# Moving loads behind a weight's bits, and four small moves at the start, in a Mamba-2 + gated MLP kernel

## The chip, the cores and the metric

The kernel runs on one core of a Trainium2 chip. The metric is the device time of one execution in microseconds. The names of the engines in the profile: PE is TensorE's matmul, PEld its weight load, DVE is VectorE, ACT is ScalarE, POOL is GpSimd, SP is SyncE, which issues nearly all DMAs here. L12 is line 12 of the kernel.

## What is computed

The reference is a chunked scan (Mamba-2, "SSD") over 4 batches x 8 heads x 768 positions with head size 32 and state size 16, then an MLP over the 3072 tokens (256 to 2048 to 256) with the quick form of Gelu between.

```python
def _attn_ref(x, a, B, C):                   # cut: set-up of shapes
    log_a = np.log(np.clip(a, 1e-06, 1.0))
    for c in range(nc):                      # chunks; xc, Bc, Cc, la are their slices
        cum = np.cumsum(la, axis=-1)
        L = np.exp(cum[:, :, :, None] - cum[:, :, None, :]) * causal
        CB = np.einsum('bhin,bhjn->bhij', Cc, Bc)
        y_intra = np.einsum('bhij,bhjd->bhid', CB * L, xc)
        y_inter = np.einsum('bhin,bhnd->bhid', Cc, state) * np.exp(cum)[:, :, :, None]
        y[:, :, sl] = y_intra + y_inter
        # ... state = decay of the whole chunk * state + sum_j decay_from_j * B_j x_j

def _moe_ref(x, w_in, w_out):                # x: y as (tokens, 256)
    h = x @ w_in
    g = h * (1.0 / (1.0 + np.exp(-1.702 * h)))
    return (g @ w_out).astype(np.float32)
```

The weights w_in and w_out come as 64-bit floats and are turned into 32-bit ones on the chip.

## The kernel before

The kernel takes the sequence in chunks of 128 positions, two chunks to a "pair" (12 pairs), two pairs to a group of 512 tokens (6 groups). A pair goes through these steps: `load` its B, C and x; `turn_only` (TensorE transposes B and C, another engine copies them out of PSUM); decays `L` (for pairs 0 and 1 by `differ` and `exps`: sums of logarithms on TensorE, Exp on ScalarE; later by scans on the DVE); `ends` (B times the decay to the chunk's end); `score` and `weigh` (C B^T, and its product with L); `gain` and `keep` (the new states); `finish` (y, two copies by ScalarE). Then the MLP: `half` and `hidden` (y times w_in, Silu), `project_all` (times w_out) for group 0, other forms for later groups, which use sums of weight blocks that `mix_in` makes. Every engine takes its instructions in the order in which the program names them (`in_order`).

Each weight comes in pieces of 64-bit words: 6 pieces of w_in (0 to 5), 4 of w_out (6 to 9). A piece goes through `fields` (DVE), `clamp` (ScalarE), `rounded` (DVE) and `join` (DVE), and join issues the load of the next piece into a buffer that has come free.

```python
    def load(p, queue=nc.sync):
        rb[p] = raw.tile([P, 2, NH, N], FP32, tag="b", name=f"b{p}", bufs=3)
        rc[p] = raw.tile([P, 2, NH, N], FP32, tag="c", name=f"c{p}", bufs=3)
        rx[p] = raw.tile([P, 2, NH, D], FP32, tag="x", name=f"x{p}", bufs=3)
        for dst, src in ((rb, B), (rc, C), (rx, x)):
            for k in range(2):
                b, c = divmod(2 * p + k, NC)
                sl = slice(c * P, (c + 1) * P)
                (queue if dst is rc else nc.sync).dma_start(out=dst[p][:, k], in_=src[b, :, sl, :].rearrange("h s d -> s h d"))
    # ...
    BUFS = 4
    bits, pieces = {}, {}
    # ... fetch(i): one DMA on nc.sync into a buffer of words(); pieces 0 and 1 share one, 2 and 3 too

    def fields(i):
        hi, cols = bits[i][1], slice(0, PIECES[i][2] * DM)
        mantissa[i] = wide.tile([P, PN], U32, tag="m", name=f"m{i}")[:, cols]
        power[i] = wide.tile([P, PN], U32, tag="p2", name=f"p2{i}")[:, cols]
        nc.vector.tensor_scalar(out=power[i], in0=hi, scalar1=0x7FF00000, scalar2=None,
                                op0=ALU.bitwise_and)
        nc.vector.tensor_scalar(out=mantissa[i], in0=hi, scalar1=0x000FFFFF,
                                scalar2=0x00100000, op0=ALU.bitwise_and, op1=ALU.bitwise_or)

    def clamp(i):
        e = power[i]
        z = e.bitcast(FP32)
        nc.scalar.activation(z, e, AF.Relu, scale=-8.0, bias=edge[:, 0:1])
        nc.scalar.activation(e, z, AF.Relu, scale=-1.0, bias=edge[:, 1:2])
    def rounded(i):
        nc.vector.scalar_tensor_tensor(out=mantissa[i].bitcast(FP32), in0=bits[i][0],
                                       scalar=2.0 ** -32, in1=mantissa[i],
                                       op0=ALU.mult, op1=ALU.add)

    NEXT = {1: (6,), 4: (7,), 5: (8,), 7: (9,)}
    def join(i):
        # ... L184: sign bits into p2 (reads the last of bits[i]); L190: product into w_in or w_out
        for n in NEXT.get(i, ()):
            fetch(n)

    def narrow(i):
        rounded(i)
        if i + 1 < len(PIECES):
            fields(i + 1)
        join(i)

```

The loads at the start, all in one queue, and the constant `idents` (the identity, 8 times, for the scans):

```python
    rows_a(az0, (nc.sync, nc.scalar))
    # ...
    load(0, nc.scalar)
    table(AF.Ln)
    fetch(0)
    load(1)
    for i in range(1, 4):
        fetch(i)
    rows_a(az, (nc.sync,))
    for i in range(4, 6):
        fetch(i)
    load(PG)
    spread_rows(1)
    # spread_rows(b): af, the raw a of batch b, for `since`; spread(n): a of chunk n from scratch
```

Copies of the transposed B and C. C goes to CT twice (Q = 2), each time times one column of `part`, a mask:

```python
        def copy(engine, o, i, scale=1.0):
            if engine == "ACT":
                nc.scalar.activation(o, i, AF.Copy, scale=scale)
            else:
                nc.vector.tensor_single_scalar(out=o, in_=i, scalar=scale, op=ALU.mult)

        s["BT"] = ssd.tile([P, 2, P], FP32, tag="BT", name=f"BT{p}")
        copy(engines[0], s["BT"], tp[:, 0])

        s["CT"] = ssd.tile([P, 2, Q, P], FP32, tag="CT", name=f"CT{p}")
        for q in range(Q):
            copy(engines[1], s["CT"][:, :, q], tp[:, 1], part[:, q:q + 1])
        s["tp"] = tp[:, 1]
        if p < PG:
            copy(engines[2], s["tp"], tp[:, 1])          # C itself, for CsT (pairs 0 and 1)
```

The order of the work at the start (`weigh` is L547, `keep` L579 and L586, `gain` L564, `half` L665 and L669; y's copies in `finish` are L631):

```python
    differ(0, [(r, ab[0, r]) for r in range(R)])
    exps(0, range(R))
    turn_only(0, ("DVE", "DVE", "DVE"))
    since_exp()
    fields(0)
    clamp(0)
    rounded(0)
    score(0, ab0)
    differ(1, [(r, ab[1, r]) for r in range(2)])
    exps(1, range(2))
    nc.gpsimd.tensor_tensor(out=own, in0=same[:, :HB], in1=same[:, HB:], op=ALU.add)
    ends(0, 0, nc.gpsimd)
    ends(0, 1, nc.gpsimd)
    weigh(0)
    turn_only(1, ("ACT", "ACT", "ACT"))
    gain(0)
    for r in range(2, R):
        ab[1, r] = bank(f"ab1_{r}")
        mask(ab[1, r])
    differ(1, [(r, ab[1, r]) for r in range(2, R)])
    exps(1, range(2, R))
    table(AF.Silu)
    since_start(0, nc.gpsimd)
    since_start(1, nc.gpsimd)
    nc.gpsimd.tensor_copy(idents, ident.unsqueeze(1).to_broadcast([P, NH, P]))
    keep(0)
    join(0)
    fields(1)
    rounded(1)
    score(1)
    ends(1, 0)
    ends(1, 1)
    weigh(1, (0,))
    finish(0)
    clamp(1)
    gain(1)
    keep(1, (0,))
    half(0, 0)
    weigh(1, (1,))
    finish(1, late=True)
    join(1)
    fields(2)
    clamp(2)
    half(1, 0)
    keep(1, (1,))
    load(PG + 1)
```

The end of y and of the first projection:

```python
    # finish(p): products y[t] (L600, L609), then
        to = early_y if p == 0 else yT[g][:, :, cols]
        for t in range(NK):
            nc.scalar.activation(to[:, t], y[t].rearrange("p k i -> p (k i)"), AF.Copy)
        if p == 0:
            nc.gpsimd.tensor_copy(yT[g][:, :, cols], to)
    # project_all: f = 0 to 15, each first the work hung in, then four products o[..] (L763); then
        for half in range(2):
            ob = out_tile(g, half)
            nc.vector.tensor_single_scalar(out=ob, in_=o[half], scalar=1.0 / GELU_SCALE,
                                           op=ALU.mult)
            store(g, half, ob)
```

What is hung into the hidden products and the projection of group 0, cut to the loads, the bits and `mix_in`:

```python
    for i, k in ((2, 1), (3, 3), (4, 4), (5, 6)):
        at(in_hidden[0], k, lambda i=i: narrow(i), lambda i=i: i < 5 and clamp(i + 1))
    at(in_hidden[0], 5, store_a)
    # store_a: clips a and writes it to scratch
    # ... k = 8, 9: pick_a(PG), clamp(6), fan_all(PG) (decays of pair 2, L384)
    at(in_hidden[0], 11, since_fanned, lambda: narrow(6))
    at(in_hidden[0], 15, lambda: clamp(7))
    for k in range(2):
        at(in_hidden[0], 5 + k, lambda k=k: spread(CG + 2 + k))
    # ...
    at(in_project[0], 9, lambda: narrow(9))
    # ...
    at(in_project[0], 14, lambda: finish(PG + 1))
    for i in range(2):
        at(in_project[0], 14, lambda i=i: mix_in(i))
    for k in range(PG):
        at(in_project[0], 8 + k, lambda k=k: load(2 * PG + k))
    for k, i in enumerate((9, 11, 13, 15)):
        at(in_project[0], i, lambda k=k: spread(2 * CG + k))
    # ... group 1:
    at(after, "H7", lambda: mix_in(2), lambda: mix_in(3))
```

Of the kernel before, what the change touches and what calls it, by code (L numbers as in the profile page):

```python
# [11 lines left out]
AF = mybir.ActivationFunctionType  # L12
ALU = mybir.AluOpType
# [3 lines left out]
P = 128  # L17
# [18 lines left out]
def kernel(  # L36
# [74 lines left out]
# [9 lines that stand above are left out]
# [51 lines left out]
# [5 lines that stand above are left out]
# [44 lines left out]
    def spread_rows(b):  # L220
        raf[b] = raw.tile([P, NC, P], FP32, tag="af", name=f"af{b}", bufs=1)
        nc.sync.dma_start(out=raf[b].rearrange("p c s -> p (c s)"),
                          in_=a[b].unsqueeze(1).to_broadcast([NH, N, S]))
# [13 lines left out]
    def table(f):  # L237

        nc.scalar.activation(early, early, f)
# [7 lines left out]
    rows_a(az, (nc.sync,))  # L247
    for i in range(4, 6):
        fetch(i)
    load(PG)  # L250
    spread_rows(1)


    edge = const.tile([P, 2], FP32, name="edge")
# [233 lines left out]
    def turn_only(p, engines=("ACT", "ACT", "ACT")):  # L488
        s = st[p] = {}
        tp = bank(f"tp{p}").rearrange("p (j k i) -> p j k i", j=2, k=2)  # L490
        for j, src in enumerate((rb[p], rc[p])):
            for k in range(2):
                nc.tensor.transpose(out=tp[:, j, k], in_=src[:, k].rearrange("p h n -> p (h n)"),  # L493
                                    identity=ident)
# [8 lines that stand above are left out]
        copy(engines[0], s["BT"], tp[:, 0])  # L503

        s["CT"] = ssd.tile([P, 2, Q, P], FP32, tag="CT", name=f"CT{p}")
        for q in range(Q):
            copy(engines[1], s["CT"][:, :, q], tp[:, 1], part[:, q:q + 1])
        s["tp"] = tp[:, 1]
        if p < PG:

            s["tp"] = ssd.tile([P, 2, P], FP32, tag="CsT", name=f"C{p}", bufs=3)
            copy(engines[2], s["tp"], tp[:, 1])
# [29 lines left out]
    def weigh(p, ks=(slice(0, 2),)):  # L542

        L, cb = Ls[p], st[p]["cb"]
        Lv = L.rearrange("p k r q i -> p k r (q i)")
        for k in ks:
            nc.vector.tensor_tensor(out=Lv[:, k], in0=Lv[:, k],  # L547
                                    in1=cb.rearrange("p r k e -> p k r e")[:, k], op=ALU.mult)
# [369 lines left out]
    def exps(p, rs):  # L918
        for r in rs:
            decay_exp(p, r, ab[p, r])  # L920
# [11 lines left out]
        mask(idle)  # L932
    differ(0, [(r, ab[0, r]) for r in range(R)])
    exps(0, range(R))
    turn_only(0, ("DVE", "DVE", "DVE"))
    since_exp()
    fields(0)
    clamp(0)
    rounded(0)
    score(0, ab0)  # L940
    differ(1, [(r, ab[1, r]) for r in range(2)])
    exps(1, range(2))
# [1 line left out]
    ends(0, 0, nc.gpsimd)  # L944
    ends(0, 1, nc.gpsimd)
    weigh(0)
    turn_only(1, ("ACT", "ACT", "ACT"))
    gain(0)
    for r in range(2, R):
# [1 line left out]
        mask(ab[1, r])  # L951
    differ(1, [(r, ab[1, r]) for r in range(2, R)])
    exps(1, range(2, R))
    table(AF.Silu)
    since_start(0, nc.gpsimd)
    since_start(1, nc.gpsimd)
    nc.gpsimd.tensor_copy(idents, ident.unsqueeze(1).to_broadcast([P, NH, P]))
    keep(0)
    join(0)
    fields(1)  # L960
    rounded(1)
    score(1)
    ends(1, 0)
    ends(1, 1)
    weigh(1, (0,))
    finish(0)
    clamp(1)
    gain(1)
    keep(1, (0,))
    half(0, 0)  # L970
    weigh(1, (1,))
    finish(1, late=True)
    join(1)
    fields(2)
    clamp(2)
    half(1, 0)
    keep(1, (1,))
    load(PG + 1)


    def at(places, i, *work):
# [17 lines left out]
    at(in_hidden[0], 15, lambda: clamp(7))  # L999
    for k in range(2):  # L1000
        at(in_hidden[0], 5 + k, lambda k=k: spread(CG + 2 + k))
    at(in_project[0], 0, lambda: turn_only(PG), lambda: narrow(7), lambda: since_start(PG))
    at(in_project[0], 1, lambda: advance(PG), lambda: clamp(8), lambda: decay(CG + 2))
    at(in_project[0], 4, lambda: scores(PG), lambda: narrow(8))
# [3 lines left out]
    at(in_project[0], 9, lambda: narrow(9))  # L1008
    at(in_project[0], 10, lambda: advance(PG + 1), lambda: scores(PG + 1))
    at(in_project[0], 14, lambda: finish(PG + 1))  # L1010
    for i in range(2):
        at(in_project[0], 14, lambda i=i: mix_in(i))
    for k in range(PG):
        at(in_project[0], 8 + k, lambda k=k: load(2 * PG + k))
# [22 lines left out]
    for k in range(CG):  # L1037
        at(after, f"P{k}", lambda k=k: decay(3 * CG + k))
        at(after, "H1" if k < 2 else "H3", lambda k=k: spread(3 * CG + k))
    at(after, "H7", lambda: mix_in(2), lambda: mix_in(3))  # L1040
    at(after, "P3", lambda: clip_rows(2), lambda: decay_rows(2), lambda: turn(p))
    at(after, "P4", lambda: mix_y(2), lambda: advance(p), lambda: turn(p + 1))
    at(after, "P5", lambda: advance(p + 1))
# [140 lines left out]
```

## Time and profile before

| | before |
|---|---|
| time, median of 3 runs | 378.24 us (377.25 to 378.48) |
| span of the profiled execution | 375.2 us |
| granted TensorE clock | 0.999 |
| DVE busy, 0 to 40 us in four tens | 4.31, 9.78, 9.67, 8.75 us |
| TensorE busy, the same | 8.61, 9.10, 9.83, 10.00 us |
| DMA busy share, the same | 0.98, 0.99, 0.84, 0.91 |
| DVE busy, 80 to 90 us | 6.35 us |

A matmul of 32-bit floats shows as two records. The records of TensorE overlap and their ends are modelled, so its busy time alone doesn't tell whether it runs at its peak; the list of its waits and the starts of its products tell more. A line of a timeline gives start, duration, engine, line and operation, out<-in, shapes, the number of instructions merged, and in brackets the idle time before it with the instruction that ended it.

### The profile page before, as it was taken

What the parts mean: (1) busy time and instruction counts of PE and PEld (TensorE: products, weight loads), DVE (VectorE), ACT (ScalarE), POOL (GpSimd) and SP (SyncE); (2) the same over time, 40 slices, a digit from 0 to 9 for tenths busy, and PEclk for the clock granted to TensorE, in tenths of its full rate; (3) what the DMA queues carried; (4) which work ended last, traced back from release to release, by engine and by line L of the source; (5) the groups of instructions that cost most, each with busy time, mean ns of one, the idle gap of its engine ahead of it and who ended that gap; (6) DMA issues with size and microseconds to landing.
All of it is one profiled execution on the core that took longest, in us unless ns stands there. A gap on an engine that the chain in (4) does not pass through costs nothing.

```text
span 375.2 us, 5771 instructions
## 1 busy us (share of the span) xinstructions
PE 367.2 (98%) x2280; PEld 284.8 (76%) x2280; DVE 268.2 (71%) x439; ACT 152.3 (41%) x337; POOL 12.4 (3%) x35
## 2 busy tenths in 40 slices
PE   8999999999999999999999999999999999999995
PEld 4674458886457678788888878888878888888884
DVE  3999899996879998677887565888574355544343
ACT  5769562403421122453423554333454331554330
POOL 4400000100000010000000000000000000000000
PEclk9999999999999999999999999999999999999999
DMA  9988888615947100077200064000010000000011
GB/s 152 235 258 194 182 307 114 190 64 91 198 93 166 59 19 23 2 142 139 112 3 0 1 114 113 0 2 0 0 58 2 0 3 1 0 2 0 0 58 56
DMA packets 85794, 29.56 MB, mean 79 GB/s; under 512 B 75720, under 2 KB 79240, under 8 KB 85768
## 3 DMA queue, kind: packets, MB, share of 16 engines
q1 hardware_dynamic: 83320, 28.81, 32.8%
q10 hardware_dynamic: 2448, 0.39, 0.6%
q8 instruction: 18, 0.29, 0.3%
q14 instruction: 8, 0.07, 0.1%
HBM read 25.95 MB, written 3.24 MB: 78 GB/s over the span
## 4 chain that ended last, share of the span: by engine, by line
PE 87%; DVE 8%; DMA 2%; issue 1%; ACT 1%; DVEq 0%; ACTq 0%
PE acc L820 32%; PE X L723 15%; PE Y L733 11%; PE o L763 8%; PE h L651 7%; PE cb L536 3%; PE y L609 3%; DMA bits<-in_moe_w_out_dram 2%; PE y L600 2%; PE tp L493 1%; DVE L L547 1%; DVE L L384 1%; PE oT L854 1%; DVE p L184 1%; PE h L665 1%
## 5 line engine op out<-in xcount | busy, mean ns | idle before, releaser
L820 PE MATMUL acc<-mg,mw 128*128 128x256 f32 x240 | 65.3, 379 | 0.0
L728 ACT ACTIVATE ac<-X 128x256 f32<-128x256 f32 x64 | 24.6, 384 | 68.9 <-PE X L723 68.8
L820 PEld LDWEIGHTS acc<-mg,mw 128*128 128x128 f32 x240 | 45.6, 190 | 6.2
L651 PE MATMUL h<-yT,w_in 128*128 128x512 f32 x112 | 50.0, 595 | 0.0
L837 DVE TENSOR_TENSOR gT<-Y,ac 128x512 f32<-128x512 f32 x32 | 22.1, 692 | 38.0 <-PE Y L733 34.9
L700 ACT ACTIVATE gT<-gT 128x512 f32<-128x512 f32 x64 | 33.3, 521 | 28.5 <-DVE gT L837 28.5
L820 PE MATMUL acc<-gT,w_out 128*128 128x256 f32 x160 | 43.8, 380 | 0.0
L349 DVE TENSOR_TENSOR_SCAN L<-a,idents 128x1024 f32<-128x1024 f32 x18 | 41.1, 2283 | 0.0
L723 PE MATMUL X<-my,mi 128*128 128x256 f32 x128 | 38.7, 384 | 0.0
L651 PEld LDWEIGHTS h<-yT,w_in 128*128 128x128 f32 x112 | 20.8, 190 | 23.4 <-issue 22.4
L820 PEld LDWEIGHTS acc<-gT,w_out 128*128 128x128 f32 x160 | 30.1, 190 | 5.4 <-issue 1.4
L837 DVE TENSOR_TENSOR gT<-Y,b 128x256 f32<-128x256 f32 x32 | 13.5, 421 | 28.0 <-PE Y L733 27.7
L654 ACT ACTIVATE gT<-h 128x512 f32<-128x512 f32 x28 | 16.6, 596 | 39.6 <-PE h L651 39.5
L763 PE MATMUL o<-w_out,gT 128*128 128x256 f32 x128 | 29.4, 384 | 0.6 <-DVE w_out L190 0.6
L547 DVE TENSOR_TENSOR L<-L,cb 128x2048 f32<-128x2048 f32 (+1 forms) x12 | 25.3, 2109 | 6.2 <-PE cb L536 6.2
L691 DVE TENSOR_TENSOR mg<-gT 128x512 f32<-128x512 f32 x40 | 27.3, 683 | 1.9 <-ACT gT L700 1.9
L763 PEld LDWEIGHTS o<-w_out,gT 128*128 128x128 f32 x128 | 23.7, 190 | 4.9 <-issue 1.1
L723 PEld LDWEIGHTS X<-my,mi 128*128 128x128 f32 x128 | 23.8, 190 | 4.2 <-issue 1.2
L820 PE MATMUL acc<-gT,mw 128*128 128x256 f32 (+1 forms) x86 | 24.0, 368 | 0.4 <-DVE c L837 0.4
L820 PE MATMUL acc<-mg,w_out 128*128 128x256 f32 x80 | 23.5, 379 | 0.0
L631 ACT ACTIVATE yT<-y 128x256 f32<-128x256 f32 x22 | 7.2, 381 | 37.6 <-PE y L609 36.3
L733 PE MATMUL Y<-yT,mi 128*128 128x256 f32 x64 | 19.5, 386 | 0.0
(145 smaller groups left out, 543.4 us busy)
## 6 DMA issues: line engine op xcount, KB each, us to landing
a<-scratch SPq DMA_DIRECT2D x18, 512.0 KB, 5.3
bits<-in_moe_w_out_dram SPq DMA_DIRECT2D x4, 1024.0 KB, 7.0
x<-in_x_dram SPq DMA_DIRECT2D x24, 128.0 KB, 3.2
out_dram<-ob SPq DMA_DIRECT2D x11, 256.0 KB, 2.2
bits<-in_moe_w_in_dram SPq DMA_DIRECT2D x4, 512.0 KB
bits<-in_moe_w_in_dram SPq DMA_DIRECT2D x2, 1024.0 KB
b<-in_B_dram SPq DMA_DIRECT2D x24, 64.0 KB, 3.9
c<-in_C_dram SPq DMA_DIRECT2D x22, 64.0 KB, 2.9
```

Of the source, the lines that this page charges most:

```text
L349: nc.vector.tensor_tensor_scan(out=Ls[p][:, k].rearrange("p r q i -> p (r q i)"), data0=ra[n], data1=idents.rearrange("p h i -> p (h i)"), ...
L547: nc.vector.tensor_tensor(out=Lv[:, k], in0=Lv[:, k], in1=cb.rearrange("p r k e -> p k r e")[:, k], op=ALU.mult)
L651: nc.tensor.matmul(out=h, lhsT=w_in[:, k, f * P:(f + 1) * P], rhs=yT[g][:, k], start=(k == 0), stop=(k == NK - 1))
L654: nc.scalar.activation(gT[g, j][:, i], h, AF.Silu, scale=GELU_SCALE)
L691: nc.vector.tensor_tensor(out=t[:, 0:2], in0=B[:, :, 1], in1=B[:, 0], op=ALU.subtract)
L700: nc.scalar.activation(o, i, AF.Silu, scale=GELU_SCALE)
L723: nc.tensor.matmul(out=s["X"], lhsT=lhsT, rhs=rhs, start=i == "1", stop=i == "4", skip_group_check=True)
L728: nc.scalar.activation(copy, s["X"], AF.Copy)
L733: nc.tensor.matmul(out=o, lhsT=lhsT, rhs=rhs, start=s.pop("new", False), stop=i != "5", skip_group_check=True)
L763: nc.tensor.matmul(out=o[k // 2][:, k % 2], lhsT=gT[g, f // 2][:, f % 2, k * P:(k + 1) * P], rhs=w_out[:, f], start=(f == 0 and k % 2 == 0 ...
L820: nc.tensor.matmul(out=acc[g][0][i][:, cols], lhsT=lhsT, rhs=rhs[:, cols], start=(j == 0 and i in (0, 2, 5, 6)), stop=(j == NF // 2 - 1), ...
L837: nc.vector.tensor_tensor(out=o, in0=v, in1=w, op=ALU.add)
```

## The change

Six moves. (1) The loads of B, C, x of pair 2 and of a of batch 1 are issued after `join(1)`, and so behind piece 6, the first of w_out, which join(1) issues; the loads of pair 3 are issued with the spreads of a, behind piece 8. The purpose is that the bits of w_out needn't stand in the queue behind loads that are needed later. (2) Where the DVE copies C (pair 0), one product with broadcast operands writes both copies. (3) `idents` is made by the DVE, before the first copies of B, in place of GpSimd, later. (4) On the DVE, `rounded(0)` goes behind weigh(0), and `rounded(1)` behind the last weigh of pair 1. (5) Silu's table is loaded behind the copies of the first y and clamp(1), not ahead of them. (6) mix_in(2) and (3) join the first two at the end of group 0's projection.

```diff
--- before.py
+++ after.py
@@ -247,8 +247,6 @@
     rows_a(az, (nc.sync,))
     for i in range(4, 6):
         fetch(i)
-    load(PG)
-    spread_rows(1)
 
 
     edge = const.tile([P, 2], FP32, name="edge")
@@ -503,8 +501,13 @@
         copy(engines[0], s["BT"], tp[:, 0])
 
         s["CT"] = ssd.tile([P, 2, Q, P], FP32, tag="CT", name=f"CT{p}")
-        for q in range(Q):
-            copy(engines[1], s["CT"][:, :, q], tp[:, 1], part[:, q:q + 1])
+        if engines[1] == "DVE":
+            nc.vector.tensor_tensor(
+                out=s["CT"], in0=tp[:, 1].unsqueeze(2).to_broadcast([P, 2, Q, P]),
+                in1=part.unsqueeze(1).unsqueeze(3).to_broadcast([P, 2, Q, P]), op=ALU.mult)
+        else:
+            for q in range(Q):
+                copy(engines[1], s["CT"][:, :, q], tp[:, 1], part[:, q:q + 1])
         s["tp"] = tp[:, 1]
         if p < PG:
 
@@ -932,11 +935,11 @@
         mask(idle)
     differ(0, [(r, ab[0, r]) for r in range(R)])
     exps(0, range(R))
+    nc.vector.tensor_copy(idents, ident.unsqueeze(1).to_broadcast([P, NH, P]))
     turn_only(0, ("DVE", "DVE", "DVE"))
     since_exp()
     fields(0)
     clamp(0)
-    rounded(0)
     score(0, ab0)
     differ(1, [(r, ab[1, r]) for r in range(2)])
     exps(1, range(2))
@@ -944,6 +947,7 @@
     ends(0, 0, nc.gpsimd)
     ends(0, 1, nc.gpsimd)
     weigh(0)
+    rounded(0)
     turn_only(1, ("ACT", "ACT", "ACT"))
     gain(0)
     for r in range(2, R):
@@ -951,31 +955,31 @@
         mask(ab[1, r])
     differ(1, [(r, ab[1, r]) for r in range(2, R)])
     exps(1, range(2, R))
-    table(AF.Silu)
     since_start(0, nc.gpsimd)
     since_start(1, nc.gpsimd)
-    nc.gpsimd.tensor_copy(idents, ident.unsqueeze(1).to_broadcast([P, NH, P]))
     keep(0)
     join(0)
     fields(1)
-    rounded(1)
     score(1)
     ends(1, 0)
     ends(1, 1)
     weigh(1, (0,))
     finish(0)
     clamp(1)
+    table(AF.Silu)
     gain(1)
     keep(1, (0,))
     half(0, 0)
     weigh(1, (1,))
     finish(1, late=True)
+    rounded(1)
     join(1)
+    load(PG)
+    spread_rows(1)
     fields(2)
     clamp(2)
     half(1, 0)
     keep(1, (1,))
-    load(PG + 1)
 
 
     def at(places, i, *work):
@@ -999,6 +1003,7 @@
     at(in_hidden[0], 15, lambda: clamp(7))
     for k in range(2):
         at(in_hidden[0], 5 + k, lambda k=k: spread(CG + 2 + k))
+    at(in_hidden[0], 6, lambda: load(PG + 1))
     at(in_project[0], 0, lambda: turn_only(PG), lambda: narrow(7), lambda: since_start(PG))
     at(in_project[0], 1, lambda: advance(PG), lambda: clamp(8), lambda: decay(CG + 2))
     at(in_project[0], 4, lambda: scores(PG), lambda: narrow(8))
@@ -1008,7 +1013,7 @@
     at(in_project[0], 9, lambda: narrow(9))
     at(in_project[0], 10, lambda: advance(PG + 1), lambda: scores(PG + 1))
     at(in_project[0], 14, lambda: finish(PG + 1))
-    for i in range(2):
+    for i in range(4):
         at(in_project[0], 14, lambda i=i: mix_in(i))
     for k in range(PG):
         at(in_project[0], 8 + k, lambda k=k: load(2 * PG + k))
@@ -1037,7 +1042,6 @@
     for k in range(CG):
         at(after, f"P{k}", lambda k=k: decay(3 * CG + k))
         at(after, "H1" if k < 2 else "H3", lambda k=k: spread(3 * CG + k))
-    at(after, "H7", lambda: mix_in(2), lambda: mix_in(3))
     at(after, "P3", lambda: clip_rows(2), lambda: decay_rows(2), lambda: turn(p))
     at(after, "P4", lambda: mix_y(2), lambda: advance(p), lambda: turn(p + 1))
     at(after, "P5", lambda: advance(p + 1))
```

## The prediction

> **What bounds the kernel now.** I read the page's busy times first, then who made TensorE wait, then the timelines of the single engines in the first 60 us, which is all the change touches apart from one move near 128 us. The page, and below it the complete list of TensorE's recorded waits:
>
> ```profile
> span 375.2 us, 5771 instructions
> PE 367.2 (98%) x2280; PEld 284.8 (76%) x2280; DVE 268.2 (71%) x439; ACT 152.3 (41%) x337; POOL 12.4 (3%) x35
> ```
>
> ```profile
> PE busy L375 <- DVE ones L258: 1.2, 1, 1.2
> PE o L763 <- DVE w_out L190: 0.6, 1, 0.6
> PE ab L536 <- DVE C L500: 0.5, 1, 0.5
> PE A L564 <- DVE Be L394: 0.5, 1, 0.5
> PE acc L820 <- DVE c L837: 0.4, 1, 0.4
> PE h L665 <- DVE w_in L190: 0.2, 1, 0.2
> ```
>
> The columns are total, times and longest, in us. TensorE sets the end: all its waits together are 3.4 us, and the change adds or removes no product. So the most that can come is what stands in this list, and the first and the fifth line (start of the program, last group) are untouched. The four in between, 1.8 us, are the candidates, and each names the DVE. Their sites, from the DVE's own timeline (start, duration, instruction; the bracket is idle time before it):
>
> ```profile
> 15.84 1.20 DVE L190 SCALAR_TENSOR_TENSOR w_in<-m,p 128x512 f32<-128x512 f32 x1
> 16.96 1.25 DVE L157 TENSOR_SCALAR p<-bits 128x512 uint32<-128x512 uint32 x1
> ...
> 19.19 0.49 DVE L394 TENSOR_TENSOR Be<-b,L 128x128 f32<-128x128 f32 x2
> ...
> 23.17 0.69 DVE L190 SCALAR_TENSOR_TENSOR w_in<-m,p 128x512 f32<-128x512 f32 x1
> 23.78 0.42 DVE L157 TENSOR_SCALAR p<-bits 128x512 uint32<-128x512 uint32 x1
> ...
> 38.92 0.69 DVE L157 TENSOR_SCALAR p<-bits 128x1024 uint32<-128x1024 uint32 x1 [1.09 <-DMA bits<-in_moe_w_out_dram]
> ...
> 51.90 1.22 DVE L190 SCALAR_TENSOR_TENSOR w_out<-m,p 128x1024 f32<-128x1024 f32 x1
> ```
>
> The reader is to see two things. The same two operations take 0.69 and 0.42 us at 23 us, but 1.20 and 1.25 us at 16 us. And at 38.92 the DVE stood 1.09 us for the bits of the second weight. GpSimd, ScalarE and the DMA queue in those stretches:
>
> ```profile
> 16.43 1.50 POOL L957 COPY idents<-ident 128x1024 f32<-128x1024 f32 x1
> ```
>
> ```profile
> 17.83 1.28 ACT L239 ACT_TABLE_LOAD   x1
> 19.13 0.20 ACT L239 ACTIVATE early<-early 128x1 f32<-128x1 f32 x1
> 19.24 0.64 ACT L631 ACTIVATE y<-y 128x256 f32<-128x256 f32 x2
> ```
>
> ```profile
> 19.19 5.15 SPq L119 DMA_DIRECT2D b<-in_B_dram  x2
> 24.39 4.05 SPq L119 DMA_DIRECT2D c<-in_C_dram  x2
> 28.48 1.31 SPq L119 DMA_DIRECT2D x<-in_x_dram  x2
> 29.83 0.90 SPq L222 DMA_DIRECT2D af<-in_a_dram  x1
> 30.85 0.38 SPq L145 DMA_DIRECT2D bits<-in_moe_w_out_dram  x1
> ```
>
> The idents copy covers the two slow DVE operations. The table load holds up the copies of the first y, which TensorE had finished at 18.99. And the first bits of w_out, whose buffer was free at 23.1 (end of L184 in join(1)), were issued at 30.85 behind pair 2's loads, and landed 8.0 us later.
>
> **What the Trainium skill says.** "Advanced Engine Details and Errata", section "GPSIMD Details": the Pool engine shares a read and a write interface with the DVE, in conflict with DVE instructions in a 2-port mode or with two SBUF inputs. The trace agrees: L190 has two SBUF inputs and lost 0.51 us, L157 lost 0.83. "VectorE: DVE Perf Modes", section "The perf-mode tier table": a copy of fp32 between SBUF tiles runs at two elements a cycle at best, and with a PSUM operand fp32 runs at one. Agrees: L300, SBUF to SBUF, took 0.55 us for 768 elements, while a single-input operation from PSUM took 0.42 for 256. "ScalarE: Activation LUTs", section "What ACT_TABLE_LOAD costs": 1283 ns for a load, plus a drain of 1380 ns. The load agrees (1.28 us); the drain isn't to be seen, since Exp ended at 17.81 and the load began at 17.83. "DMA: Bandwidth & Descriptors", section "Queues, rings and completion order": an engine takes the descriptors of a ring in order, so what is queued first goes first. The trace before shows only this one order.
>
> **The change part by part.**
>
> Start, up to TensorE's half(1,0) at 24.00. From 10.36 to 18.99 TensorE runs without a recorded gap (scores of pair 0, decays of pair 1, scores of pair 1, first y). The first of these waited for the last Exp of ScalarE (four of about 0.5 us from 8.25, end 10.32) as well as for the DVE's C copies. Making two C copies (0.78 us together) into one product of 512 elements (0.69, the duration of such a product from PSUM in L837) thus doesn't bring it forward: 0 us. The idents copy goes into the DVE's 2.05 us of idle time ahead of 8.81. It takes 0.6 to 1.2 us for 1024 elements, by L300's rate or at one a cycle: 0 us.
>
> DVE after that. weigh(0) no longer stands behind rounded(0): it needs the scores (end 11.53) and GpSimd's two Be (end 11.51), so it starts at 11.6, not 11.98, and ends at 13.87. Then rounded(0) 0.60, to 14.47; keep(0) from 14.47 (before 14.25); join(0) and fields(1), free of idents, end about 17.5, though GpSimd's CsT product (15.77 to 16.50) still runs beside join(0). Be of pair 1 waits for ScalarE's last Exp (17.81): start 17.86, where it was 19.19. From there the DVE runs: Be 0.4, weigh(1,0) 18.25 to 19.38, keep 0.6 to 20.05, weigh(1,1) 1.13 to 21.18, rounded(1) 0.60, and join(1) 0.62 + 0.70 to 23.10 (before 23.86). With the handover of 0.14 half(1,0) can start at 23.24.
>
> TensorE beside it. y(0) ends at 18.99 as before. gain(1) follows at once (before 19.53), since Be is there. ScalarE, with no table load ahead, copies y from about 18.85, as at pair 2, where the copies began 0.93 after the first of its L609. half(0,0) starts at 19.4 instead of 19.98 and ends at 21.3; y(1) takes 0.42 + 1.01 + 0.48 and ends at 23.2. DVE and TensorE arrive together at 23.25. **Gain 0.75 us.** The table load, now after clamp(1) (19.5 to 21.0), ends near 22.4, and the first Silu can have its input at 21.3: it begins about 0.4 later than before (22.02), but its bank isn't asked for until half(1,0) at 23.2.
>
> 23 to 53 us. TensorE runs on with nothing recorded but the wait at 53.27. The closest case is the weight for hidden(0,8), ready at 35.89 and used at 36.13; both move by 0.75, so the gap stays. Bits of w_out: issued at about 22.5 behind w_in's last pieces (landed by 30.85), 1 MB at the 400 GB/s or so that the DMA view shows in its best slices is 2.6 us, so landed about 33.5. The DVE asks for them at 37.83 - 0.4 = 37.4. The 1.09 wait goes. The DVE is then 1.5 us earlier, so w_out's first piece is ready near 51.6, and TensorE wants it at 52.66 - 0.75 = 51.9. **Gain 0.61 us**, all of the wait, since TensorE can win no more there than it waited.
>
> After 53 us. mix_in(2) and (3), 8 x 0.37 = 2.94 us of DVE, move from 128 us into the 3.42 us that the DVE stood ahead of the output copy at 87.59. They fit with about 0.5 us to spare. At 128 to 131 the DVE loses that load, but TensorE shows no wait there: 0 us.
>
> Sum: 378.24 - 0.75 - 0.61 = 376.88, told as 376.9.
>
> **The rivals.**
>
> First, ScalarE or TensorE instead of the DVE in the first 24 us. If the copies of y(0) start only when TensorE is quite done, half(0,0) comes at 19.77, y(1) ends at 23.56, and the start gains 0.4: about 377.2. For it: the shift of y(0) is none, and 0.2 us of slack is all there is. Against: the copies at pair 2 began while the last products ran.
>
> Second, a transfer takes the place of the old wait. Loads of pairs 2 and 3 now come 10 us later; b of pair 2 is asked for at 45.6, b of pair 3 at about 59.7, and the queue has two megabyte pieces and two spreads ahead of pair 3. The short rows are slow: issuing pair 2 took 10.6 us (19.19 to 29.83). Should they land late, the DVE stands and TensorE with it, and the 0.6 us goes back or more: 377.5 to 379. For it: the DMA engines are busy 0.77 to 0.91 of the time from 30 to 60 us. Against: pair 2 should land near 36 and pair 3 by 55, some 5 us and more ahead, and the scratch writes that held up later spreads no longer wait for pair 3.
>
> Third, the DVE at 88 us: if mix_in doesn't fit, the output copies free their banks late and TensorE waits at hidden(1): up to 1 us, 377.9. Against: 2.94 is less than 3.42.
>
> Fourth, more than the sum: if the first scores waited on C rather than on Exp, TensorE moves 0.1 to 0.2 us forward from 10.36: 376.7.
>
> **Range and chances.** Single runs of before lie 1.2 us apart, as much as the gain. The range from 375.9 to 378.2 holds the sum, the first and the third rival and that spread. A change of 2% is 7.6 us; TensorE waits only 3.4 in all, so faster by that has 0.01, slower by that needs a long DMA stall, 0.01, and the rest, 0.98, is within 2%.
>
> **What would show it.** L190 and L157 in the first 24 us at about 0.7 and 0.4; the first y copy near 18.9; half(1,0) near 23.25; the DVE without a wait for w_out's bits, and TensorE's list without L763's and L564's lines. Wrong would be a new wait in that list: for b, x or a spread between 45 and 75 us, or for the output copies near 87; also a half(1,0) that still starts at 23.6 or later, or a gap left at the first w_out product.

## The result, and the profile after

The changed kernel takes 375.71 us (median of 6 runs, 375.62 to 376.32), the kernel before 377.81 in the same comparison (6 runs, 377.25 to 378.48): ratio 0.9947, 95% interval 0.9934 to 0.9961, so 2.1 us less. The prediction of 376.9 with a range from 375.9 to 378.2 had the direction right; the time fell 0.2 us below the range.

The profiled execution of the changed kernel took 376.32 us, the longest of its six; that of the kernel before took 377.17, less than any of its six. The two traces are therefore nearer to each other (spans 374.6 and 375.2) than the medians. The page after (its last line here is the chain of work that ended last, in shares of the span):

```profile
span 374.6 us, 5767 instructions
...
PE 367.4 (98%) x2280; PEld 285.0 (76%) x2280; DVE 267.5 (71%) x439; ACT 152.3 (41%) x337; POOL 10.6 (3%) x34
...
PE 94%; DVE 3%; ACT 1%; issue 1%; DVEq 0%; ACTq 0%
```

Of the page before, the line like the last of these:

```profile
PE 87%; DVE 8%; DMA 2%; issue 1%; ACT 1%; DVEq 0%; ACTq 0%
```

TensorE's recorded waits after, the complete list (total, times, longest, in us):

```profile
PE busy L373 <- DVE ones L256: 1.2, 1, 1.2
PE ab L539 <- ACT L L474: 0.6, 1, 0.6
PE h L668 <- DVE w_in L190: 0.4, 1, 0.4
PE acc L823 <- DVE c L840: 0.4, 1, 0.4
```

(L392 is ends, which makes Be, L474 the Exp of exps, L539 score, L567 gain, L582 and L589 keep, L636 GpSimd's copy to yT, L668 half, L766 the products with w_out, L772 the output copy.) Two lines of before are gone: the first w_out product (0.6) and gain's (0.5). The scores wait 0.56, before 0.55, now for ScalarE's last Exp in place of the DVE's C copies. half's wait grew from 0.2 to 0.4. TensorE has 94% of the chain that ended last, before 87%, and the DMA no longer stands in it. The DVE's timeline at the places that the prediction named (start, duration, instruction; idle time before it in brackets):

```profile
6.91 0.68 DVE L938 COPY idents<-ident 128x1024 f32<-128x1024 f32 x1
...
16.82 1.10 DVE L190 SCALAR_TENSOR_TENSOR w_in<-m,p 128x512 f32<-128x512 f32 x1
17.84 0.41 DVE L157 TENSOR_SCALAR p<-bits 128x512 uint32<-128x512 uint32 x1
...
18.57 0.49 DVE L392 TENSOR_TENSOR Be<-b,L 128x128 f32<-128x128 f32 x2
...
20.43 0.61 DVE L589 SCALAR_TENSOR_TENSOR S<-S,since,S 128x128 f32<-128x128 f32 x1
20.96 1.21 DVE L550 TENSOR_TENSOR L<-L,cb 128x1024 f32<-128x1024 f32 x1
22.09 0.68 DVE L173 SCALAR_TENSOR_TENSOR m<-bits,m 128x512 f32<-128x512 uint32 x1
22.69 0.68 DVE L184 SCALAR_TENSOR_TENSOR p<-bits,p 128x512 uint32<-128x512 uint32 x1
23.41 0.69 DVE L190 SCALAR_TENSOR_TENSOR w_in<-m,p 128x512 f32<-128x512 f32 x1
...
37.98 0.69 DVE L157 TENSOR_SCALAR p<-bits 128x1024 uint32<-128x1024 uint32 x1
...
86.08 0.42 DVE L688 TENSOR_TENSOR mi<-w_in,mi 128x256 f32<-128x256 f32 x1
86.99 0.69 DVE L772 TENSOR_SCALAR ob<-o 128x512 f32<-128x512 f32 x1 [0.49 <-PE o L766]
```

```profile
21.05 0.35 DVE L586 SCALAR_TENSOR_TENSOR S<-S,since,S 128x128 f32<-128x128 f32 x1
```

fields(1) (L157 at 17.84) fell from 1.25 to 0.41 us, but join(0) (L190 at 16.82) only from 1.20 to 1.10, and keep's L589 at 20.43 rose from 0.35 (L586 in the line of before below) to 0.61. At 37.98 the DVE finds the bits there, where it had stood 1.09 us. Ahead of the output copy at 86.99 it has 0.49 us left of 3.42. GpSimd, ScalarE and the DMA queue beside it:

```profile
16.48 0.89 POOL L524 TENSOR_TENSOR CsT<-C,since 128x256 f32<-128x256 f32 x1 [3.89 <-ACT C L496]
20.28 0.61 POOL L636 COPY yT<-y 128x512 f32<-128x512 f32 x1 [2.91 <-ACT y L634]
```

```profile
17.45 1.09 ACT L474 ACTIVATE L<-ab 128x512 f32<-128x512 f32 x2 [1.11 <-PE ab L455]
19.56 0.66 ACT L634 ACTIVATE y<-y 128x256 f32<-128x256 f32 x2 [1.03 <-PE y L612]
...
21.60 1.28 ACT L239 ACT_TABLE_LOAD   x1
```

```profile
23.40 0.37 SPq L145 DMA_DIRECT2D bits<-in_moe_w_out_dram  x1
23.81 3.05 SPq L119 DMA_DIRECT2D b<-in_B_dram  x2
```

The two slow operations of the DVE lie beside a GpSimd instruction each: L190 beside the CsT product, L589 beside the copy to yT. The first of the two cost the chain nothing: Be of pair 1 (L392, at 18.57) has to wait for ScalarE's last Exp (end 18.54) in any case. The table load stands behind the y copies, and the bits are issued ahead of pair 2's loads. TensorE's timeline around the first w_out product, before and then after:

```profile
52.06 0.38 PE L493 MATMUL tp<-ident,b 128*128 128x128 f32 x2
52.28 0.38 PE L493 MATMUL tp<-ident,c 128*128 128x128 f32 x2
53.27 1.10 PE L763 MATMUL o<-w_out,gT 128*128 128x256 f32 x4 [0.61 <-DVE w_out L190]
```

```profile
52.31 0.38 PE L491 MATMUL tp<-ident,b 128*128 128x128 f32 x2
52.52 0.38 PE L491 MATMUL tp<-ident,c 128*128 128x128 f32 x2
52.74 1.46 PE L766 MATMUL o<-w_out,gT 128*128 128x256 f32 x6
```

From the start of the last transposes to the start of the product it was 0.99 us, and is now 0.22: 0.77 us less, where the recorded wait is 0.61, since that is counted from a modelled end.

**The accounts of the two traces.** The scores of pair 0 start at 10.36 before and at 11.08 after. Nothing in the change delays them: kernels of both kinds, below, start them anywhere from 9.93 to 11.12. When a landed and how long the first products took differ between them too. So I count from the scores. half(1,0) follows 13.64 us behind them before (24.00) and 13.17 after (24.25): 0.47 gained. The w_out product follows at 42.91 and at 41.66: 1.25 in all, and with 0.07 won within its next products the span is 1.32 us shorter for equal starts. From hidden(1,0) to the end it is 286.95 us in both.

### The profile page after: what moved, and what is told of

Same layout as the page of the kernel before. It is cut to its first block, busy times and chain, and to the rows that moved or that the text cites. A ratio compares the mean times of both kernels' runs of the same rounds, so it can differ in the third digit from the quotient of the medians.

```text
span 374.6 us, 5767 instructions
## 1 busy us (share of the span) xinstructions
PE 367.4 (98%) x2280; PEld 285.0 (76%) x2280; DVE 267.5 (71%) x439; ACT 152.3 (41%) x337; POOL 10.6 (3%) x34
## 4 chain that ended last, share of the span: by engine, by line
PE 94%; DVE 3%; ACT 1%; issue 1%; DVEq 0%; ACTq 0%
PE acc L823 32%; PE X L726 15%; PE h L654 13%; PE Y L736 11%; PE o L766 8%; PE cb L539 3%; PE y L612 3%; PE y L603 2%; PE h L668 1%; PE tp L491 1%; DVE L L550 1%; PE oT L857 1%; PE A L567 1%; PE ab L447 1%; PE ab L455 1%
## 5 line engine op out<-in xcount | busy, mean ns | idle before, releaser
L766 PE MATMUL o<-w_out,gT 128*128 128x256 f32 x128 | 29.3, 383 | 0.0
L766 PEld LDWEIGHTS o<-w_out,gT 128*128 128x128 f32 x128 | 23.8, 190 | 4.1 <-issue 0.7
```

The lines of the kernel that those rows point to most:

```text
L766: nc.tensor.matmul(out=o[k // 2][:, k % 2], lhsT=gT[g, f // 2][:, f % 2, k * P:(k + 1) * P], rhs=w_out[:, f], start=(f == 0 and k % 2 == 0 ...
```

## The experiments

Every text quoted names its own theories. What was open: (a) why the start brought 0.47 and not 0.75; (b) whether the wait of w_out is a fixed 0.61 us or a floor set by the landing of the bits, which takes away what is gained ahead of it; (c) where the rest of the 2.1 us is. A comparison runs each kernel beside the kernel before; medians of before differ from comparison to comparison, so the ratios are compared, not the times.

**The two kernels again** (e4 is before; e3 and e13 are after). No edit.

> The kernel before unchanged. Both: ratio 1.000. What its profile settles: under theory A the DVE's wait for the first w_out bits is different from the 1.09 us of the first profile, longer in a longer run, and the gap ahead of L763 follows it; under theory B it is 1.09 again and a longer run is longer before 24 us.

> The changed kernel unchanged. Both theories: 2.1 us faster than before, 375.7 us. What its profile settles: whether the late start of the profiled run (first scores at 11.08 instead of 10.36) comes back. Theory A says that it was that run's landing of a, so scores near 10.36 and a span near 374.0; theory B that part of the change delays or hastens the start, so 11.08 again.

> The changed kernel unchanged, beside the mended one. The first comparison gave it 2.1 us over before, the second 1.2. Theory A (what varies is how late w_out's bits land in before): before's median differs between the comparisons more than the changed kernel's, which stays at 375.6 to 376.1.

The kernel before against itself: 376.97 us (13 runs), ratio 1.0003 (0.9989 to 1.0018). In its profiled execution the DVE waited 0.42 us for the bits, not 1.09, and TensorE has no recorded wait at the w_out product. The changed kernel: 376.01 (20 runs) against 377.01 (48 runs), 0.9968 (0.9958 to 0.9978), and once more 375.69 (5 runs), 0.9966 (0.9954 to 0.9979). So the gain in repeats is 1.2 to 1.3 us, not the 2.1 that was expected of e3. Between the three comparisons the median of before moved by 0.80 us (377.81, 377.01, 377.19), that of the changed kernel by 0.32. The scores started at 9.93 and 10.35, half(1,0) 13.16 to 13.17 later, the w_out product 41.66 later in both, as in the first trace.

**The loads alone, and everything but the loads.** The first is the kernel before with part 1; the second is the changed kernel with the loads at their old places.

```diff
 # e1: before, with
-    load(PG)                      # ahead of the constants
-    spread_rows(1)
     join(1)
+    load(PG)
+    spread_rows(1)
     keep(1, (1,))
-    load(PG + 1)
     for k in range(2):
         at(in_hidden[0], 5 + k, lambda k=k: spread(CG + 2 + k))
+    at(in_hidden[0], 6, lambda: load(PG + 1))
 # e2: after, with the reverse of these lines
```

> The kernel before with the moved loads alone (part 1). Theory A, the wait for w_out's bits is the larger part and differs from run to run: about 1.4 us faster than before by the medians (0.85 us that the gap ahead of the first w_out product measures in the profiled runs, and some 0.6 us more that an ordinary run of before waits); half(1,0) starts as in before, 13.6 us after the first scores, and the gap ahead of L763 is gone. Theory B, the surplus comes from the start: only about 0.85 us faster.

> The changed kernel with the loads of pairs 2 and 3 back at their old places. Theory A: within 0.2 us of before although half(1,0) comes about 0.5 us earlier, because the first w_out product then waits for the same landing, and the gap there grows by as much. Theory B: 1.2 us faster than before.

The loads alone: 376.55 us, ratio 0.9985 (0.9975 to 0.9994), or 0.6 us faster, less than either theory said. The w_out product stands 42.14 us behind the scores (10.76, 52.90) and has no wait in the list. Everything but the loads: 376.92, ratio 0.9998 (0.9987 to 1.0009), though half(1,0) came 13.17 behind the scores as in the changed kernel. From that kernel's timelines, DVE and TensorE:

```profile
38.88 0.69 DVE L157 TENSOR_SCALAR p<-bits 128x1024 uint32<-128x1024 uint32 x1 [1.59 <-DMA bits<-in_moe_w_out_dram]
```

```profile
53.23 1.97 PE L768 MATMUL o<-w_out,gT 128*128 128x256 f32 x8 [1.11 <-DVE w_out L190]
```

The start was gained and lost again: the DVE came earlier and waited 1.59 us in place of 1.09, TensorE 1.11 in place of 0.61, and the product began at the same time as before (53.23 and 53.27). That is a floor, not a fixed wait. The parts don't add: 0.6 and 0.1 us alone, 1.2 together.

**Is the floor the landing?** Four more executions of the kernel before (e15 to e18), no edit:

> The kernel before, one profiled execution. Theory A: the first w_out product starts at the later of TensorE's arrival (42.1 us after the first scores) and 14.3 us after the DVE gets w_out's first bits, and the execution ends 322 us after it; in a longer execution it is the bits that come later. Theory B: the bits come at the same time in every execution (38.6 to 38.9), and a longer one is longer elsewhere.

> The same once more, for another draw of the start and of the landing: theory A and theory B as in the look before.

> The same once more: theory A and theory B as in the look before.

> The same once more: theory A and theory B as in the look before.

| execution | scores | fields(6) begins | wait for the bits | scores + 42.14 | fields(6) + 14.35 | w_out product | time |
|---|---|---|---|---|---|---|---|
| first trace | 10.36 | 38.92 | 1.09 | 52.50 | 53.27 | 53.27 | 377.17 |
| e4 | 10.76 | 38.64 | 0.42 | 52.90 | 52.99 | 53.00 | 376.88 |
| e15 | 10.72 | 39.31 | 1.12 | 52.86 | 53.66 | 53.67 | 377.56 |
| e16 | 11.08 | 38.46 | none | 53.22 | 52.81 | 53.21 | 377.04 |
| e17 | 10.63 | 38.42 | 0.32 | 52.77 | 52.77 | 52.78 | 376.68 |
| e18 | 11.12 | 38.50 | none | 53.26 | 52.85 | 53.26 | 377.08 |

The two constants are from e1 and from the first trace (so its row agrees by construction); in that trace the DVE works through the 14.2 us from fields(6) to the end of the weight without a recorded wait. The later of the two columns gives the product within 0.01 us each time, also in e16 and e18, where the bits were not waited for and the DVE was held by its own work. The landing moves by 0.9 us from execution to execution, TensorE's arrival by 0.8, and the time follows the later one. So theory A's formula holds; that the longer executions come from late bits alone doesn't: e15 was long by its bits, e16 and e18 by their start. The DVE's lines of e15 and e16:

```profile
39.31 0.69 DVE L157 TENSOR_SCALAR p<-bits 128x1024 uint32<-128x1024 uint32 x1 [1.12 <-DMA bits<-in_moe_w_out_dram]
```

```profile
38.46 0.69 DVE L157 TENSOR_SCALAR p<-bits 128x1024 uint32<-128x1024 uint32 x1
```

Then the queue itself: two transfers of 64 KB in the short rows of C, read by nobody, ahead of the bits in the kernel before (e11), and behind them in the changed one (e12).

```diff
     load(PG)
+    spare = dram.tile([2, NH, P, N], FP32, name="spare")
+    for k in range(2):
+        nc.sync.dma_start(out=spare[k].rearrange("h s d -> s h d"),
+                          in_=C[3, :, k * P:(k + 1) * P, :].rearrange("h s d -> s h d"))
     spread_rows(1)
```

> The kernel before with two more transfers of short rows (64 KB each, from C to a spare place in DRAM, read by nobody) ahead of w_out's first bits. Theory A, the landing of these bits is the bound of before: each microsecond that they land later comes out at the end; I expect 3 to 5 us later, and a time 3 to 5 us longer, with TensorE's wait ahead of L763 as much longer. Rival, the wait at L763 isn't on the path (the lost time is won back before 88 us): the same time as before.

> The changed kernel with the same two spare transfers of C as in the run with more ahead of the bits, here behind w_out's first bits, after pair 2's loads. Theory A: none of the 1.0 us that they cost in before; the DVE has no wait for the first bits, and the time is the changed kernel's. Rival, the spare transfers cost by loading the DMA engines, wherever they stand: 0.5 us or more above it.

e11: 378.48 us, ratio 1.0038 (1.0025 to 1.0050). I had expected the bits 3 to 5 us later; the DVE got them at 39.63, 0.3 to 1.2 us later than in the six executions above, and the time went up by 1.4 us in the ratio (0.0038 of 377). The two took 1.78 us to issue, where the two C loads just ahead of them took 4.01; why is not shown. The queue's line, the DVE's and TensorE's:

```profile
29.26 1.78 SPq L253 DMA_DIRECT2D spare<-in_C_dram  x2
```

```profile
39.63 0.69 DVE L157 TENSOR_SCALAR p<-bits 128x1024 uint32<-128x1024 uint32 x1 [1.37 <-DMA bits<-in_moe_w_out_dram]
```

```profile
53.98 1.97 PE L766 MATMUL o<-w_out,gT 128*128 128x256 f32 x8 [0.88 <-DVE w_out L190]
```

39.63 + 14.35 is 53.98. e12: 375.92, ratio 0.9970 (0.9957 to 0.9982), product 41.67 behind the scores: the same transfers behind the bits cost nothing. What stands ahead of the bits in the queue sets the floor.

**What held the start back.** e8 takes part 4 back (rounded(0) and rounded(1) at their old places); e9 takes the copy to yT from GpSimd and gives it to ScalarE behind half(1,0); e10 does both.

```diff
 # e8: after, with (lines between left out)
     clamp(0)
+    rounded(0)
     weigh(0)
-    rounded(0)
     fields(1)
+    rounded(1)
     finish(1, late=True)
-    rounded(1)
     join(1)
 # e9: after, with
         if p == 0:
-            nc.gpsimd.tensor_copy(yT[g][:, :, cols], to)
+            pass
     half(1, 0)
+    nc.scalar.activation(yT[0][:, :, :2 * P], early_y, AF.Copy)
```

> The changed kernel with rounded(0) and rounded(1) back at their old places on the DVE. Theory: in the changed kernel half(1,0) waits 0.40 us for the DVE; rounded(0) stands idle-free behind weigh(0) while the DVE waits 0.91 us ahead of it, so the move lengthens the DVE's chain by 0.6 us. Undone, half(1,0) starts when TensorE arrives, 12.77 us after the first scores instead of 13.17, and the time is 0.4 us below the changed kernel. Rival, the move is what brought the half microsecond: half(1,0) 13.4 or later, time 0.3 us or more above it.

> The changed kernel with GpSimd's copy of the first y into yT made by ScalarE instead, behind half(1,0)'s Silu. Theory, that copy collides with the DVE's L589 and costs it 0.26 us: L589 takes 0.35 instead of 0.61, half(1,0) starts 12.9 us after the first scores, the time is 0.25 us below the changed kernel. Rival, L589 is long for another reason (its operand S from PSUM's product): 0.61 and 13.17 as in the changed kernel.

> The changed kernel with both mends: rounded(0) and (1) at their old places, and yT copied by ScalarE. Theory, TensorE is the bound once the DVE no longer is: half(1,0) 12.8 us after the first scores, as with the first mend alone, so 0.4 us below the changed kernel and no better than with one mend. Rival, the two add up: 12.5 and 0.65 us below.

e8: 375.38 us, ratio 0.9958 (0.9942 to 0.9974); e9: 375.45, 0.9958 (0.9943 to 0.9973); e10: 375.47, 0.9959 (0.9947 to 0.9972). half(1,0) stands 12.79, 12.90 and 12.80 us behind the scores (13.17 in the changed kernel), the w_out product 41.29, 41.40 and 41.29 (41.66). Both mends together bring no more than e8. TensorE has no recorded wait at half(1,0) in the three. TensorE's line of e8 and the DVE's of e9:

```profile
23.09 1.10 PE L668 MATMUL h<-y,w_in 128*128 128x256 f32 x4
```

```profile
19.90 0.35 DVE L589 SCALAR_TENSOR_TENSOR S<-S,since,S 128x128 f32<-128x128 f32 x1
```

With no GpSimd copy beside it L589 takes 0.35 us, not 0.61: the collision is shown. join(1)'s product (L190) begins 12.33 us behind the scores in the changed kernel, 12.06 in e9, 11.96 in e10 and 11.95 in e8. So the collision costs 0.27, and the new order of the rounded operations another 0.10 without it: with the new order Be of pair 1 starts 7.49 us behind the scores (7.48 in e9), as soon as ScalarE's last Exp is over, and with the old one, behind rounded(1), at 7.98 (e8). So the move wins 0.50 ahead of Be and pays 0.60 for rounded(1) behind it. With the old order the collision is gone too, since the DVE comes to L589 at 20.13, when GpSimd's copy (19.50 to 20.11) is over. That is why e10 gains nothing over e8: its DVE chain is no shorter (11.96 and 11.95), and half(1,0) starts 0.84 behind L190 in both, as in the changed kernel. The theory of e10 had the number right for another reason. The change's part 4 lengthens the chain that it was to shorten.

**idents back on GpSimd** (e5). The changed kernel without part 3:

```diff
-    nc.vector.tensor_copy(idents, ident.unsqueeze(1).to_broadcast([P, NH, P]))
     turn_only(0, ("DVE", "DVE", "DVE"))
     since_start(1, nc.gpsimd)
+    nc.gpsimd.tensor_copy(idents, ident.unsqueeze(1).to_broadcast([P, NH, P]))
```

> The changed kernel with idents made by GpSimd again, behind the CsT products. Theory: L190 about 1.2 and L157 about 1.2 us on the DVE near 17 us, Be of pair 1 about 1.1 us later, half(1,0) 14.2 us after the first scores, the time 1.1 us above the changed kernel. Rival, the collision lies in slack: 13.2 and the same time.

376.50 us, ratio 0.9989 (0.9981 to 0.9997): without this part most of the gain is gone. half(1,0) stands 13.70 behind the scores, the w_out product 42.20, or 0.54 more than in the changed kernel. The ratios differ by about 0.8 us; 0.22 of the rest lies outside the span, below. GpSimd's line and the DVE's:

```profile
16.56 1.50 POOL L959 COPY idents<-ident 128x1024 f32<-128x1024 f32 x1
```

```profile
16.07 1.10 DVE L190 SCALAR_TENSOR_TENSOR w_in<-m,p 128x512 f32<-128x512 f32 x1
17.09 1.25 DVE L157 TENSOR_SCALAR p<-bits 128x512 uint32<-128x512 uint32 x1
```

Only L157 pays for idents (1.25, 0.41 without); L190 has its 1.10 in both. GpSimd's CsT product stands beside it in every run, and no run moved that; e19, below, is the kernel before without the idents copy on GpSimd, and has:

```profile
15.79 1.19 DVE L190 SCALAR_TENSOR_TENSOR w_in<-m,p 128x512 f32<-128x512 f32 x1
```

I had expected half(1,0) later still, 14.2 behind the scores; but the later DVE comes to L589 when the copy to yT is over, and L589 takes 0.35.

**Table, mix_in and C copies back** (e14). The changed kernel without parts 2, 5 and 6:

```diff
-        if engines[1] == "DVE":
+        if False:                 # two copies of C again
     exps(1, range(2, R))
+    table(AF.Silu)
     clamp(1)
-    table(AF.Silu)
-    for i in range(4):
+    for i in range(2):
         at(in_project[0], 14, lambda i=i: mix_in(i))
+    at(after, "H7", lambda: mix_in(2), lambda: mix_in(3))
```

> The changed kernel with three of its moves undone at once: Silu's table ahead of the first y's copies, mix_in(2) and (3) near 128 us, two copies of C. Theory: the y copies come 0.45 us later, half(0,0) 0.4 us later, but half(1,0) waited 0.40 us for the DVE anyway: 13.2 us after the first scores, the same time within 0.1 us. Rival, the table counts in full: 13.6 and 0.4 us above the changed kernel.

375.74 us, ratio 0.9969 (0.9956 to 0.9983), w_out product 41.61 behind the scores: the three parts are worth nothing on this path. The table load does delay TensorE at half(0,0), 9.30 behind the scores in place of 8.92, but half(1,0) still comes at 13.08, slightly earlier than in the changed kernel. There the collision is gone: GpSimd's copy to yT begins at 20.11, L589 at 19.88, and L589 takes 0.35. What the later table wins for the y copies, the collision that it brings takes back:

```profile
19.82 1.99 PE L668 MATMUL h<-y,w_in 128*128 128x256 f32 x8 [0.44 <-ACT y L634]
```

**Outside the span.** Time and span of every execution are known. Time minus span lies between 1.88 and 2.01 us in all 157 executions so far of the kernels with the idents copy on GpSimd (before, e1, e5, e11), mean 1.94, and between 1.67 and 1.79 in all 75 of the others (after, e2, e8 to e10, e12, e14), mean about 1.72. Some 0.22 us of the gain is in no trace. Either the idents copy costs it, or the number of GpSimd's instructions: 35 before and 34 after (33 in e9, which has no less). e19 is the kernel before with idents moved alone; e20 is the changed kernel with a memset of GpSimd that nobody reads.

```diff
 # e19: before, with
+    nc.vector.tensor_copy(idents, ident.unsqueeze(1).to_broadcast([P, NH, P]))
     turn_only(0, ("DVE", "DVE", "DVE"))
-    nc.gpsimd.tensor_copy(idents, ident.unsqueeze(1).to_broadcast([P, NH, P]))
 # e20: after, with
     since_start(1, nc.gpsimd)
+    spare = const.tile([P, 6], FP32, name="spare")
+    nc.gpsimd.memset(spare, 0.0)
```

> The kernel before, with only the copy of idents moved to the DVE. In every execution of the kernels whose idents copy is on GpSimd (before and two variants) the time was 1.88 to 2.01 us longer than the recorded span, in every execution of the others 1.67 to 1.79. Theory A (the move itself saves about 0.22 us outside the span): time minus span 1.72. Theory B (something else in the change does): 1.95. Inside the span: L157 at 17 us 0.42 in place of 1.25, half(1,0) at the scores + 13.1 in place of + 13.64, but the first w_out product still held by the bits (their fields(6) + 14.35), so the span shortens by 0 to 0.5 us. Time against before: A -0.2 to -0.7 us, B 0 to -0.5.

> The changed kernel with one more instruction for GpSimd, a memset of 128x6 read by nobody, where the idents copy used to stand. If the number of GpSimd's instructions sets the 0.22 us outside the span (35 before, 34 after; against it: the variant with 33 has no less), time minus span is 1.94; if it is the copy of idents that costs it, 1.72. Span as of the changed kernel: first w_out product at the scores + 41.66.

e19: time minus span 1.72 (20 runs, 1.67 to 1.79), the kernel before beside it 1.94 (32 runs). e20: 1.95 (13 runs, 1.90 to 2.00), with its w_out product 41.67 behind the scores as ever. GpSimd's line of e20:

```profile
16.77 0.10 POOL L961 MEMSET spare<- 128x6 f32 x1
```

A memset of 0.10 us brings the whole 0.22 back, so it isn't the copy of idents but one GpSimd instruction more. (It stands where the copy stood; whether the place counts, and not the number alone, wasn't tried.) The difference between 33 and 34 is nil (e9), between 34 and 35 it is 0.22. What happens there, before the first or after the last recorded instruction, isn't shown.

e19's time was 376.41, ratio 0.9991 (0.9980 to 1.0002), and it shows the floor once more: half(1,0) stood 13.07 behind the scores, 0.57 better than before, and the bits took all of it. TensorE would have been there at 51.88 (13.07 and the 28.50 that lie between half(1,0) and the product in e1), but 38.20 + 14.35 is 52.55:

```profile
52.55 1.97 PE L763 MATMUL o<-w_out,gT 128*128 128x256 f32 x8 [0.48 <-DVE w_out L190]
```

e20 as a whole: 376.08, ratio 0.9975 (0.9965 to 0.9985).

## Why the prediction was right and wrong

**The step that failed** is "Gain 0.61 us, all of the wait, since TensorE can win no more there than it waited". It took a wait that one execution showed for a fixed size. The runs show a floor: the product starts at the later of TensorE's arrival and the bits + 14.35 us. Three things follow from that. First, with the loads out of the way, the 0.61 is worth 0.85 in the same pair of traces (0.78 from half(1,0) to the product, 0.07 in the next products). Second, it is not one number: in six executions of the kernel before TensorE was held there by 0 to 0.8 us against its arrival. Third, the 0.61, read in an execution of 377.17, was taken from a base of longer ones, 378.24. The range was made on the same error: it set the spread of before against the gain, but counted neither that the base of three runs lies in that spread nor that the change takes a part of the spread away. Of 48 runs of the kernel before in one comparison seven lie above 377.9, and the 378.24 is such a value. These long executions go with the old place of the loads. In kernels with the loads there (before, e2, e4, e19) 28 of 180 runs lie more than 0.75 us above the median of their kernel and comparison, the longest 1.95 (e4). In kernels with the loads moved none of 108 does, the longest 0.71 (e12).

**The start** was one term with the wrong size: 0.75 predicted, 0.47 measured. Up to Be of pair 1 the predicted chain of the DVE holds: 7.50 us behind the scores, measured 7.49. L190 of join(0), whose excess was put down to the idents copy, kept 1.10 of its 1.20 (and 1.19 in e19), but that is over by the end of ScalarE's Exp. Behind Be two steps were longer. The y copies, moved earlier, brought GpSimd's copy to yT beside L589, +0.26, of which the predicted chain had 0.07 to spare (keep at 0.6 us, from 19.38 to 20.05). And from L184 to L190 0.72 us go by, in the trace before too (22.45 to 23.17), where the chain had 0.62. The first is the conflict for which the prediction cites the Trainium skill, "Advanced Engine Details and Errata", "GPSIMD Details", on operations with two SBUF inputs; it was applied to the idents copy and to no other. (That L589 has two SBUF inputs is in the kernel: the old and the new state. L157 has one, so that it falls under that sentence only if it ran in a 2-port mode, which no trace shows.) Moreover the later rounded operations, counted as a gain, were a loss (e8, e10).

**"The idents copy: 0 us"** failed by 0.22 outside the span (e19, e20). No timeline shows it; time minus span does.

**The sum.** Predicted: 0.75 + 0.61 = 1.36. Found in the traces and outside: 0.47 + 0.85 + 0.22 = 1.54. Repeats of the comparison gave 1.2 and 1.3, with intervals of about 0.4 to either side, so all three agree. That 1.36 does is in part luck: its start was 0.28 too large, its floor 0.24 too small, and the 0.22 was missing. The first comparison gave 2.1. Of the 1.17 us between 376.88 and 375.71, 0.43 is the base (378.24 of three runs, 377.81 of six) and 0.18 is 1.54 less 1.36. The other 0.56 is in that comparison alone. Late bits in its six runs of before would explain it, and the long executions above speak for them; late starts do so less, since e18, with the latest (11.12), took 377.08. But no trace is that long: as an estimate, 378.24 needs the bits at 40.0 (less the 323.9 from the product on in the first trace, less 14.35), and the latest of before were at 39.31 (e15). That stays open. So does whether the scores start 0.3 us earlier in the kernels derived from the changed one by more than chance.

**Right:** the DVE does not wait for the bits, nor TensorE for w_out. The y copies began 0.93 us behind the first of y's products, so the first rival (copies late) is false. No load of pair 2 or 3 came late; there is no DMA in TensorE's list, the second rival is false. mix_in fits with 0.49 us to spare where about 0.5 was predicted, the third is false. The single product for C frees nothing, as the scores still wait for Exp; the fourth is false. Idents took 0.68 us of idle DVE time. The bits were issued at 23.40, which is the predicted 22.5 and most of the 0.72 by which this execution started late.

## What to carry to other kernels

A wait for a transfer is a floor: it swallows what is gained ahead of it (e2: half(1,0) 0.47 us earlier behind the scores, product at the same time), so move the transfer first, and look at several executions before its length goes into a sum. When an engine is relieved or work is moved earlier, list for each interval what GpSimd does beside the DVE's operations on SBUF, since the collision moves with it (e9), and ask whether it lies in a wait: L190's in the changed kernel does and costs nothing. Take the base of a gain of 1 us from many runs, and look at time minus span as well as at the span. Here the changed kernel with part 4 taken back (e8) brings the w_out product 0.37 us nearer to the scores than the change does; it was the best by the trace, while the intervals of the ratios overlap.

## What the runs showed of the hardware

- One GpSimd instruction more (35 in place of 34) lengthened every execution by 0.22 us outside the recorded span, although it lasted 0.10 us (e20, with the instruction at one place); 33 and 34 don't differ (e9).
- L157, one SBUF input, took 0.42 us alone and 1.25 beside the 1.50 us idents copy; L190, two SBUF inputs, 0.69 alone and 1.10 to 1.20 beside GpSimd's CsT product of 0.72 to 0.91, with the idents copy behind that or without it; L589 0.35 alone and 0.61 beside a copy of 0.61. Not every overlap slows the DVE: in the changed kernel L160 at 11.11 took 0.42 beside GpSimd's Be (11.10 to 12.17).
- The bits, 1 MB behind the same loads in the queue, let the waiting DVE go on at anything from 38.20 (e19) to 39.31 us (e15). In the kernel before the first scores began at 10.36 to 11.12 (e18).
- The six bf16 products ahead of the first sums took from 1.97 us (e5) to 2.74 us (e16) with no change to them.
